# Decode block with cached attention: loops on four engines, another tail, and the query weights in eight transfers

## Chip, core and metric

The kernel runs on one NeuronCore of a Trainium2 chip. TensorE multiplies matrices into the eight banks of PSUM, VectorE (DVE) and ScalarE (ACT) work on SBUF and PSUM, GpSimd (POOL) makes a few constants, and SyncE (SP) issues almost all DMA transfers. Sixteen DMA engines move the data. The metric is the device time of one execution in microseconds (us).

## What is computed

One decoding step of a transformer block for two sequences: layer norm, attention of one query per head over a cache of 8192 keys and values, a residual, a second layer norm, a bilinear gated unit and another residual. All is float32.

```python
B, Sq, D = 2, 1, 448
H, Sk, Dh = 16, 8192, 256
F = 1792
q = (layernorm(x) @ wq).reshape(B, Sq, H, Dh).transpose(0, 2, 1, 3)
scores = einsum("bhqd,bhkd->bhqk", q, k_cache) * Dh ** -0.5
o = einsum("bhqk,bhkd->bhqd", softmax(scores), v_cache)
h = x + o.transpose(0, 2, 1, 3).reshape(B, Sq, H * Dh) @ wo
n = layernorm(h)
out = h + ((n @ w_gate) * (n @ w_up)) @ w_down
```

## The kernel before

There are 32 pairs of head and sequence, `NQ`, called heads here and numbered i. Each has 8192 keys and 8192 values of 256 floats. Partition p holds 64 consecutive keys, so a head's keys are one tile of 128 x 64 x 256 floats; so are its values. SBUF holds two key tiles (`k_sb`, even and odd heads) and one value tile (`v_sb`). Nothing is read twice, and there is no room for more of the cache.

**Start.** SP issues the query weights `wq` into the value tile (one transfer of 128 rows, L179), then head 0's keys in two pieces (16 and 48 of 64) and head 1's keys. ACT issues x. VectorE centres x, TensorE turns it, and TensorE projects the 4096 queries in eight groups of 512 columns, four matmuls each (L282), which ScalarE copies out with the norm's factor (L290). Between groups TensorE spreads the first two queries over 128 partitions with a matmul against ones (`spread_query`, L270). After the last group (`all_q`) the value tile is free, and SP issues head 0's values.

**Heads.** VectorE multiplies the keys in place by the spread query (L334) and sums over 256 columns (L337), in two pieces, then takes each partition's maximum (L381). TensorE turns these (`find_top`, L422), VectorE takes the largest (L343), TensorE spreads it (L426), and ScalarE takes the exponential with its sum (L352, L355). TensorE adds the sums up (L431), spreads the query of head i+2 (L270), mixes the values in 32 matmuls over four column groups (L413), and after ScalarE's copy (L363) turns the result (`turn_up`, L438); ScalarE scales it into `oT` (L365). Keys of head i+2 are issued when VectorE has done head i, values of head i+1 when TensorE has mixed head i. Only TensorE's heads stand in a loop (L446, 31 turns, `Fori`); VectorE, ScalarE and SP have their instructions written out one after another, and TensorE's last head too.

**Tail.** The output projection of 15 heads (`project_out`, L493, 60 matmuls over two halves of 224 columns) is done while the last values load. The last values come in 48 and 16 of 64. `sums` opens two sums in PSUM: `h_ps` for the norm and `y_ps` for the result. The last head's part is added to both (L589, L697), the total and the mean are taken (L597, L604), and the centred row is spread into `xr` (L630). Then follow the gate (L668 with `wg`), the up projection in two halves of its columns with `wu` (L668), each with its own product and flip (L717, L720, L727), and the down projection with `wd`, 14 rows of four matmuls (L738), loaded in pieces of 5, 5, 3 and 1 rows (`DOWN`). VectorE copies the result out (L747), SP stores it.

**What sets the order.** Each engine runs its instructions in the order in which they are written, and waits on counters (semaphores) of other engines and of loads. SP issues in its written order; DMA engines take transfers from its queue in that order.

Of the kernel before, what the change touches and what calls it, by code (L numbers as in the profile page):

```python
# [3 lines left out]
F32 = mybir.dt.float32  # L4
# [8 lines left out]
DC = 4  # L13
YN, YW = 4, D // 4
HW = D // 2
# [6 lines left out]
LASTV = 48  # L22
# [5 lines left out]
WIDE = [[min(n, (k + 1) * FH) - k * FH for n in FG] for k in range(2)]  # L28
PACKED = [3 * sum(n) + n[0] + n[2] for n in WIDE]
FF = [(n, g) for n in range(4) for g in range(4) if n < FG[g] // P]  # L30
DOWN = (5, 5, 3, 1)
# [8 lines left out]
class Line:  # L40


    def __init__(self, nc, engine, name):
        self.e = engine
        self.sem = nc.alloc_semaphore(name=name)
        self.n = 0
        self.seen = {}

    def wait(self, *tokens):
        for sem, n in tokens:  # L50
            if self.seen.get(sem.num, 0) < n:
                self.e.wait_ge(sem, n)
                self.seen[sem.num] = n

    def did(self, ins):
        ins.then_inc(self.sem, 1)
        self.n += 1
        return self.sem, self.n


class Tensor:


    def __init__(self, nc):
        self.e = nc.tensor
        self.sem = nc.alloc_semaphore(name="pe")
        self.n = 0
        self.parts = [(None, [])]

    def loop(self, *turns):  # L70

        self.parts.append((turns or None, []))

    def do(self, make, *waits, inc=False):
        self.parts[-1][1].append((make, waits, inc))
        if inc:
            self.n += 1
            return self.sem, self.n

    def emit(self):  # L80
        for turns, ops in self.parts:
            if turns:
                with self.e.Fori(*turns) as turn:
                    self.emit_part(ops, turn)
            else:
                self.emit_part(ops, None)

    def emit_part(self, ops, turn):
        seen = {}
        for make, waits, inc in ops:  # L90
            for w in waits:
                sem, n = w[:2]
                if len(w) == 3:
                    self.e.wait_ge(sem, turn * w[2] + n)
                elif seen.get(sem.num, 0) < n:
                    self.e.wait_ge(sem, n)
                    seen[sem.num] = n
            ins = make() if turn is None else make(turn)
            if inc:
                ins.then_inc(self.sem, 1)  # L100


def decode_block(nc, x, k_cache, v_cache, wq, wo, wg, wu, wd, out):
# [6 lines left out]
    bank = [nc.alloc_psum_tensor(f"bank{i}", [P, 512], F32)[:] for i in range(8)]  # L110
    first_sem = nc.alloc_semaphore(name="dve_first")
    V = Line(nc, nc.vector, "dve")
    A = Line(nc, nc.scalar, "act")
    A_q = Line(nc, nc.scalar, "act_q")
    G = Line(nc, nc.gpsimd, "pool")
    S = Line(nc, nc.sync, "sp")
    T = Tensor(nc)

# [3 lines left out]
    def load(line, dst, src, sem, n=16):  # L122
        line.e.dma_start(dst, src).then_inc(sem, 16)  # L123
        return sem, n
# [5 lines left out]

    room = {"at": 2 * NF * D}

    def late(*shape):

        n = 1
        for k in shape[1:]:
            n *= k
        at = room["at"]
        room["at"] += -(-n // 8) * 8
        assert room["at"] <= NJ * DH  # L140
        got = k_flat[1][: shape[0], at : at + n]
        names = "abcd"[: len(shape) - 1]
        if len(names) > 1:
            got = got.rearrange(
                f"p ({' '.join(names)}) -> p {' '.join(names)}",
                **dict(zip(names[1:], shape[2:])),
            )
        return got
# [8 lines left out]
    xr = sb("xr", P, DC + 1, B, 16)  # L157
    xz = sb("xz", P, DC + 1, B)
    sel = sb("sel", P, 2)
    rep = sb("rep", P, 2, B, REP)  # L160
    q_sb = sb("q_all", B, H * DH)

    s_x, s_wq, s_k0 = landing("x"), landing("wq"), landing("k0")
    s_k = [landing("k_even"), landing("k_odd")]
    s_v, s_v2 = landing("v"), landing("v_last")
    s_wo = [landing("wo_a"), landing("wo_b")]
    s_wg, s_wu = landing("wg"), [landing("wu_a"), landing("wu_b")]
    s_wd = [landing(f"wd{i}") for i in range(len(DOWN))]
    s_out = landing("out")

    def keys_of(cache, i, lo, hi):
        h, b = divmod(i, B)
        return cache[b, h].rearrange("(p j) d -> p j d", p=P)[:, lo:hi, :]

    x_in = load(A, x_sb, x.rearrange("b s d -> (b s) d"), s_x)
    wq_t = v_flat[:, : 3 * H * DH + H * DH // 2]
    wq_in = load(S, wq_t, wq, s_wq)  # L179
    k0_in = load(S, k_sb[0][:, :HC], keys_of(k_cache, 0, 0, HC), s_k0)  # L180
    k_in = {0: load(S, k_sb[0][:, HC:], keys_of(k_cache, 0, HC, NJ), s_k[0])}
    k_in[1] = load(S, k_sb[1], keys_of(k_cache, 1, 0, NJ), s_k[1])

    zero = G.did(nc.gpsimd.memset(ident, 0.0))
    G.wait(zero)
    ident_in = G.did(
        nc.gpsimd.affine_select(
            out=ident, in_=ident, compare_op=ALU.not_equal, fill=1.0, base=0,
            pattern=[[-1, P]], channel_multiplier=1,
        )  # L190
    )
    G.did(nc.gpsimd.memset(xz, 0.0))
    zeros_in = G.did(nc.gpsimd.memset(xr[:, DC - 1 :], 0.0))

    V.did(nc.vector.memset(eps_t, EPS))
    V.did(nc.vector.memset(ones, 1.0))
    V.did(nc.vector.memset(avg, 1.0 / D))
    V.did(nc.vector.memset(row, DH**-0.5))
    o_ps, h_ps, y_ps = bank[0], bank[5][:, :P], bank[6][:, :YW]
    V.wait(x_in)  # L200
    xsum = sb("xsum", B, 1)
    t = V.did(nc.vector.tensor_reduce(xsum, x_sb, axis=AX.X, op=ALU.add))
    V.wait(t)
    xmean = sb("xmean", B, 1)
    t = V.did(nc.vector.tensor_scalar(xmean, xsum, -1.0 / D, None, op0=ALU.mult))
    V.wait(t)
    xc_sb = sb("xc", B, DC * P)
    t = V.did(nc.vector.tensor_scalar(xc_sb[:, :D], x_sb, xmean, None, op0=ALU.add))
    V.wait(t)
    xc_in = V.did(nc.vector.tensor_copy(xc_sb[:, D:], xc_sb[:, D - HALF : D]))  # L210
    xq = o_sb[:B, :D]
    t = V.did(nc.vector.tensor_mul(xq, xc_sb[:, :D], xc_sb[:, :D]))
    V.wait(t)
    xvar = sb("xvar", B, 1)
    var_in = V.did(nc.vector.tensor_reduce(xvar, xq, axis=AX.X, op=ALU.add))

    std = sb("std", B, 1)
    A.wait(var_in)
    std_in = A.did(nc.scalar.activation(std, xvar, AF.Sqrt, bias=eps_t, scale=1.0 / D))
    rstd = sb("rstd", B, 1)  # L220
    V.wait(std_in)
    rstd_in = V.did(nc.vector.reciprocal(rstd, std))
    A.wait(rstd_in)
    A.did(nc.scalar.activation(std, std, AF.Exp, scale=0.0))

    xT_ps = bank[3][:, : DC * B].rearrange("p (c b) -> p c b", b=B)
    for c in range(DC):
        xT_in = T.do(
            lambda c=c: nc.tensor.transpose(
                xT_ps[:, c, :], xc_sb[:, c * P : (c + 1) * P], ident[:B, :B]  # L230
            ),
            ident_in, xc_in, inc=c == DC - 1,
        )
    V.wait(xT_in, zeros_in)
    for rows, c, to in LAYOUT:
        xz_in = V.did(nc.vector.tensor_copy(xz[rows, to], xT_ps[rows, c]))

    V.wait(ident_in)
    V.did(
        nc.vector.tensor_reduce(  # L240
            sel, ident.rearrange("p (g r) -> p r g", r=32)[:, :2, :], axis=AX.X, op=ALU.add
        )
    )
    V.did(
        nc.vector.tensor_copy(
            rep,
            ident.rearrange("p (k b) -> p k b", k=2)[:, :, :B, None].to_broadcast([P, 2, B, REP]),
        )
    )
    for ps in (o_ps, h_ps, bank[4][:, :HW]):  # L250
        set_in = V.did(nc.vector.memset(ps, 0.0))

    q_sel = sb("q_sel", B, DH)
    qb = [sb(f"qb{i}", P, DH) for i in range(2)]
    qb_ps = bank[1][:, :DH]
    q_ps = [bank[7][:B, :], bank[4][:B, :]]
    qsel_in, qb_in, Q_in = {}, {}, {}

    def select(i):
        h, b = divmod(i % NQ, B)  # L260
        if i > 0:
            A.wait(Q_in[i - 1])
        qsel_in[i] = A_q.did(
            nc.scalar.activation(  # L264
                q_sel, q_sb[:, h * DH : (h + 1) * DH], AF.Copy, scale=ident[:B, b : b + 1]
            )
        )

    def spread_query(*_):
        return nc.tensor.matmul(qb_ps, ones[:B, :], q_sel, start=True, stop=True)  # L270

    def take_query(i):
        A.wait(Q_in[i])
        qb_in[i] = A_q.did(nc.scalar.activation(qb[i % 2], qb_ps, AF.Copy))  # L274

    q_in = {}
    for g in range(NG):
        for c in range(DC):
            xs = c if c < DC - 1 else c + g // (NG // 2)
            at = c * H * DH + (g * QG if c < DC - 1 else g % (NG // 2) * QG)  # L280
            done = T.do(
                lambda g=g, c=c, xs=xs, at=at: nc.tensor.matmul(  # L282
# [11 lines left out]
        if g == 0:  # L294
            A.wait(q_in[0])
            select(0)
        if g == 1:
            Q_in[0] = T.do(spread_query, qsel_in[0], set_in, inc=True)
# [519 lines left out]
```

## Time and profile before

| | |
|---|---|
| median of 3 runs | 1302.37 us (1302.2 to 1302.61) |
| the profiled execution | 1301.42 us, of which the span from first to last instruction is 1300.1 us |
| bytes read | 561.19 MB, 432 GB/s over the span |
| granted TensorE clock, mean | 0.642 of full |
| first load issued | 0.73 us |
| projection of the queries done, first values issued | 53.66 us |
| last values issued | 1248.66 us |
| last down rows issued | 1275.74 us |

Times in the profile are in us from the span's start. Names such as `k` and `v` leave out the buffer's number. In the tail many small tiles lie in the key tiles, so they show as `k`; `v` stands for the value tile, which holds `wq` at the start and `wd` at the end. A float32 matmul shows as two entries of TensorE, and as two weight loads (PEld).

### The profile page before, as it was taken

Reading aid. Unit: us, or ns where it says so; the run is one execution under the profiler, and the core shown is the slowest. Engines: PE = TensorE matmul, PEld = TensorE weight load, DVE = VectorE, ACT = ScalarE, POOL = GpSimd, SP = SyncE. Lnnn points to the kernel's source line nnn. Section 1 sums busy time; section 2 is a strip of 40 time slices with the busy share of each in tenths; the row PEclk is TensorE's granted clock in tenths of the full one; section 3 lists DMA queues with packets and bytes.
Section 4 is the critical chain, followed back from the end, with each engine's and each line's share of the span. In section 5 each row is a group of like instructions: output and inputs, shape, how many; then the busy total and the mean of one; then the engine's idle time right before and its main releaser. Section 6 shows DMA issues by size and latency. Waiting matters only on the chain.

```text
span 1300.1 us, 6914 instructions
## 1 busy us (share of the span) xinstructions
PE 470.6 (36%) x2992; PEld 155.1 (12%) x2992; DVE 1131.2 (87%) x266; ACT 81.5 (6%) x239; POOL 0.8 (0%) x8
## 2 busy tenths in 40 slices
PE   3643224333323433322333322333321333432387
PEld 0111011101001101101101101101100110110123
DVE  1999998889888889888889988888988888988861
ACT  1100000000000000000000000000000000000000
POOL 0000000000000000000000000000000000000000
PEclk9866566666556666556666656666656666655689
DMA  9999999999999999999999999999999999999998
GB/s 411 427 450 421 450 421 444 426 436 436 421 450 421 448 423 448 423 446 425 442 427 427 444 421 450 422 446 425 446 423 446 425 440 429 427 444 423 446 421 367
DMA packets 10973, 561.31 MB, mean 432 GB/s; under 512 B 1234, under 2 KB 1364, under 8 KB 1492
## 3 DMA queue, kind: packets, MB, share of 16 engines
q1 hardware_dynamic: 10960, 561.19, 99.7%
q8 instruction: 5, 0.08, 0.0%
q14 instruction: 4, 0.03, 0.0%
q10 hardware_dynamic: 4, 0.00, 0.0%
HBM read 561.19 MB, written 0.00 MB: 432 GB/s over the span
## 4 chain that ended last, share of the span: by engine, by line
DMA 74%; PE 25%; issue 0%; ACT 0%; SPq 0%; DVE 0%
DMA v<-in_A_v_cache_dram 71%; PE bank L413 22%; PE bank L282 2%; DMA v<-in_wd_dram 2%; DMA v<-in_wq_dram 1%; PE bank L270 0%; SPq L123 0%; PE bank L738 0%; ACT q_all L290 0%; ACT q_sel L264 0%; DVE k L747 0%; ACT qb L274 0%
## 5 line engine op out<-in xcount | busy, mean ns | idle before, releaser
L334 DVE TENSOR_TENSOR k<-k,qb 128x4096 f32<-128x4096 f32 x64 | 555.3, 8676 | 124.2 <-DMA k<-in_A_k_cache_dram 95.9
L337 DVE TENSOR_REDUCE s<-k 128x16 f32<-128x4096 f32 x64 | 555.2, 8675 | 1.1
L413 PE MATMUL bank<-v,p 128*2 128x512 f32 x2048 | 291.4, 733 | 342.9 <-DMA v<-in_A_v_cache_dram 342.9
L413 PEld LDWEIGHTS bank<-v,p 128*2 128x2 f32 x2048 | 53.6, 96 | 573.4 <-DMA v<-in_A_v_cache_dram 365.9
L426 PE MATMUL bank<-nm,row 1*128 1x1 f32 x64 | 18.4, 354 | 227.6 <-DVE nm L343 227.6
L422 PE MATMUL bank<-ident,m 128*1 128x128 f32 x32 | 11.8, 368 | 184.4 <-DVE m L381 184.4
L363 ACT ACTIVATE o_sb<-bank 128x512 f32<-128x512 f32 x31 | 18.5, 597 | 604.0 <-PE bank L413 604.0
L426 PEld LDWEIGHTS bank<-nm,row 1*128 1x128 f32 x64 | 15.6, 302 | 236.9 <-DVE nm L343 236.9
L438 PE MATMUL bank<-sel,o_sb 128*128 128x1 f32 x256 | 33.7, 253 | 23.3 <-ACT o_sb L363 22.5
L270 PE MATMUL bank<-q_sel,ones 2*128 2x256 f32 x66 | 39.0, 691 | 1.4 <-ACT q_sel L264 1.4
L438 PEld LDWEIGHTS bank<-sel,o_sb 128*128 128x128 f32 x256 | 31.0, 191 | 53.1 <-ACT o_sb L363 51.5
L282 PE MATMUL bank<-v,xz 128*2 128x512 f32 x64 | 30.7, 639 | 16.0 <-DMA v<-in_wq_dram 16.0
L352 ACT ACTIVATE nb<-bank 128x1 f32<-128x1 f32 x32 | 5.5, 171 | 441.5 <-PE bank L426 441.5
L431 PE MATMUL bank<-lsum,ones 128*128 128x1 f32 x64 | 18.5, 359 | 23.5 <-ACT p L355 23.5
L422 PEld LDWEIGHTS bank<-ident,m 128*1 128x1 f32 x32 | 2.5, 79 | 188.2 <-DVE m L381 187.8
L431 PEld LDWEIGHTS bank<-lsum,ones 128*128 128x128 f32 x64 | 15.8, 306 | 26.2 <-ACT p L355 26.2
L270 PEld LDWEIGHTS bank<-q_sel,ones 2*128 2x128 f32 x66 | 15.9, 297 | 3.7 <-ACT q_sel L264 2.4
L264 ACT ACTIVATE q_sel<-q_all,ident 2x256 f32<-2x256 f32 x33 | 16.2, 492 | 0.0
L274 ACT ACTIVATE qb<-bank 128x256 f32<-128x256 f32 x32 | 12.2, 382 | 54.5 <-PE bank L270 54.5
L493 PE MATMUL bank<-k,oT 128*2 128x224 f32 x120 | 13.4, 387 | 0.0
L343 DVE TENSOR_REDUCE nm<-bank 1x1 f32<-1x128 f32 x32 | 8.7, 272 | 4.4 <-PE bank L422 4.4
L597 DVE TENSOR_REDUCE k<-bank 128x1 f32<-128x128 f32 x1 | 0.3, 292 | 13.1 <-PE bank L589 13.1
(81 smaller groups left out, 97.3 us busy)
## 6 DMA issues: line engine op xcount, KB each, us to landing
v<-in_wq_dram SPq DMA_DIRECT2D x1, 7168.0 KB, 19.5
k<-in_wo_dram SPq DMA_DIRECT2D x2, 3584.0 KB, 35.3
k<-in_A_k_cache_dram SPq DMA_DIRECT2D x1, 6144.0 KB, 38.0
v<-in_A_v_cache_dram SPq DMA_DIRECT2D x1, 6144.0 KB, 21.6
k<-in_wg_dram SPq DMA_DIRECT2D x1, 3136.0 KB, 28.0
v<-in_wd_dram SPq DMA_DIRECT2D x2, 1120.0 KB, 18.0
k<-in_A_k_cache_dram SPq DMA_DIRECT2D x1, 2048.0 KB, 23.9
v<-in_A_v_cache_dram SPq DMA_DIRECT2D x1, 2048.0 KB, 26.1
```

Of the source, the lines that this page charges most:

```text
L264: nc.scalar.activation(q_sel, q_sb[:, h * DH : (h + 1) * DH], AF.Copy, scale=ident[:B, b : b + 1])
L270: return nc.tensor.matmul(qb_ps, ones[:B, :], q_sel, start=True, stop=True)
L282: lambda g=g, c=c, xs=xs, at=at: nc.tensor.matmul(q_ps[g % 2], xz[:, xs, :], wq_t[:, at : at + QG], start=(c == 0), stop=(c == DC - 1),),
L334: t = V.did(nc.vector.tensor_mul(kt, kt, q[:, None, :].to_broadcast([P, hi - lo, DH])))
L337: V.did(nc.vector.tensor_reduce(s_t[i % 2][:, lo:hi], kt, axis=AX.X, op=ALU.add)),
L363: osb_in[i] = A.did(nc.scalar.activation(o_sb, o_ps, AF.Copy))
L413: lambda *_, t=t, g=g: nc.tensor.matmul(o_ps[g : g + 2, :], p_t[:, 2 * t : 2 * t + 2], v_sb[:, 2 * t : 2 * t + 2, :], start=(t < 4), stop= ...
L422: return T.do(lambda *_: nc.tensor.transpose(mT_ps, m_t, ident), m, inc=True)
L426: lambda *_: nc.tensor.matmul(nb_ps, row, nm, start=True, stop=True), nm_done, inc=True
L431: lambda *_: nc.tensor.matmul(l_ps, ones, lsum, start=True, stop=True), p_done, inc=True
L438: lambda *_, c=c, k=k: nc.tensor.matmul(oT_ps[:, c : c + 1], o_sb[:, (2 * k + c) * P : (2 * k + c + 1) * P], sel[:, k : k + 1], start=(k = ...
L493: lambda h=h, c=c, k=k: nc.tensor.matmul(acc_ps[HALF * k : HALF * k + B, :], oT[:, h, c, :], wo_c[:, h, c, k * HW : (k + 1) * HW], start=F ...
```

## The change

A class `Engine` takes the place of `Line` and `Tensor`. Work is recorded as a list for each engine, with names for what is waited for, and written out at the end. `roll` writes a body once with a loop around it; waits in it are against a register computed from the turn. `only` writes a block that is stepped over in all turns but one.

- **Loops.** TensorE: four turns over two query groups, then 32 turns over heads; the last head's extra work (`heads_out`) and one wait are blocks within the turn. VectorE: heads 1 to 30 as 15 turns of two. ScalarE: 16 turns of two. SP stays written out.
- **Query groups.** They run in the order 0, 4, 1, 5, 2, 6, 3, 7. The first query is spread inside the first turn, the second behind the loop.
- **Hints.** Each of SP, TensorE, ScalarE and VectorE gets a prefetch hint for code at its end, and a branch there that is never taken. TensorE has a second cut, `later()`, between gate and up projection: the far block gets a hint from the beginning, and is reached by a branch.
- **Query weights.** Eight transfers; transfer r holds rows r, r+8, ... of 128, sixteen rows of 57344 bytes.
- **Tail.** The 15 heads are projected 448 columns at a time over four column groups (30 matmuls and one for x); `sel` adds the groups into two halves, `half_ps`. Five filler matmuls (`keep_busy`) follow, ahead of the last mix. The last head is added to `half_ps` alone; ScalarE copies it with its row sum, and small matmuls make the centred row. The up projection runs over its full width, its loads cut by rows of the weights; the last chunk of gate and up takes 64 weight columns, in two matmuls where there were four. The first ten down rows are summed two rows high over four column groups (`part_ps`), with the residual; VectorE copies this, and four matmuls add it to `y_ps` beside the last four down rows. `DOWN` is 5, 5, 2, 1, 1. `wo` comes in one transfer, and all `wd` loads wait for the whole last mix.

```diff
-    wq_in = load(S, wq_t, wq, s_wq)
+    for r in range(8):
+        load(S, wq_t[r::8], wq[r::8], s_wq, "wq", n=8 * 16)
...
+    def emit(self, known):
+        e, nc, seen = self.e, self.nc, {}
...
+        hint = e.mark_branch_hint_location()
+        never = e.alloc_register(name + "never")
+        e.reg_mov(never, 0)
+        if self.split:
+            e.br_lt(never, 0, on_true=name + "far", on_false=name + "near").branch_hint(hint)
+            with nc.body(name + "near", valid_engines=here):
+                hint = e.mark_branch_hint_location()
+                self.emit_ops(self.items[self.ahead : self.split], known, seen)
+                nc.br(name + "far", engines=here)
+            nc.switch_bb(name + "far")
+        self.emit_ops(self.items[self.split or self.ahead :], known, seen)
+        e.br_lt(never, 0, on_true=name + "dead", on_false=name + "end")
+        with nc.body(name + "dead", valid_engines=here):
+            e.br_lt(never, 0, on_true=name + "dead", on_false=name + "end").branch_hint(hint)
...
+    def emit_turn(self, turns, steps, turn, known, seen):
+        for k, op in enumerate(turns[0]):
+            if op[0] == "only":
+                at = [j for j, t in enumerate(turns) if t[k][1]]
+                here = turn < steps[1] if at == [0] else turn > steps[-2]
+                with self.e.If(here):
+                    self.emit_ops(turns[at[0]][k][1], known, {})
+                continue
...
+                self.e.wait_ge(sem, turn * a + b if a else b)
...
+    T.roll(0, GH, 1, project_groups)
+    spread_query(1)
...
+    V.roll(1, NQ - 1, 2, lambda i: (scores(i), scores(i + 1)))
...
+    A.roll(0, H, 1, act_turn)
...
+    def heads_out():
...
+        for at in range(0, H - 1, 4):
+            for c in range(2):
+                for h in range(at, min(at + 4, H - 1)):
+                    g = 32 * (h % 4)
+                    T.do(
+                        lambda h=h, c=c, g=g: nc.tensor.matmul(
+                            acc_ps[g : g + B, :], oT[:, h, c, :], wo_c[:, h, c, :],
...
+        T.do(None, ("oT", NQ - 2))
+        T.roll(0, WARM, 1, keep_busy)
+    def keep_busy(_):
+        T.do(
+            lambda _: nc.tensor.matmul(warm_ps, ones, wo_t[:, : 2 * P], start=True, stop=True)
+        )
...
+        spread_query(i + 2)
+        T.only(last, heads_out)
+        at = 0
+        for k, n in enumerate(LAST):
+            if k > 0:
+                T.only(last, hold, ("v_last", k))
+            mix(
...
+    T.roll(0, NQ, 1, tensor_turn)
...
+    T.later()
+    project(u_ps, wu_t, lambda c: ("wu", c // 2), "u", "u_blank")
...
+    for k, (j, g) in enumerate(FF[:NPART]):
+        T.do(
+            lambda k=k, j=j, g=g: nc.tensor.matmul(
+                part_ps[32 * (k % 4) : 32 * (k % 4) + B, :],
+                hmT[:, j, 32 * g : 32 * (g + 1) : REP], wd_t[:, k, :],
+                start=(0 < k < 4), stop=(k >= NPART - 4),
+            ),
```

How the instructions now stand is shown at three places. First SP, from the top of the program: `v<-in_wq_dram` is the load of the query weights, the `k` loads are head 0's keys in two pieces and head 1's. Before:

```order
L123 DMA v<-in_wq_dram 128x14336
L123 DMA k<-in_A_k_cache_dram 128x4096
L123 DMA k<-in_A_k_cache_dram 128x12288
L123 DMA k<-in_A_k_cache_dram 128x16384
L123 DMA v<-in_A_v_cache_dram 128x16384
```

And with the change:

```order
L185 DMA v<-in_wq_dram 16x14336 x8
L185 DMA k<-in_A_k_cache_dram 128x4096
L185 DMA k<-in_A_k_cache_dram 128x12288
L185 DMA k<-in_A_k_cache_dram 128x16384
L95 BRANCH_PREFETCH_HINT
L185 DMA v<-in_A_v_cache_dram 128x16384
```

Seven more issues stand ahead of the keys, none ahead of the first weights; the hint stands behind the keys.

Second TensorE, one turn of the loop over heads. Before (`m`, `nm` and `lsum` belong to the softmax, `p` holds the exponentials):

```order
L422 MATMUL bank<-ident,m 1x128
L94 REGISTER_ALU
L426 MATMUL bank<-nm,row 128x1
L94 ISA
L431 MATMUL bank<-lsum,ones 128x1
L94 ISA
L270 MATMUL bank<-q_sel,ones 128x256
L94 ISA
L413 MATMUL bank<-v,p 2x512 x32
```

And with the change, from the spread query to the end of the mix:

```order
L379 MATMUL bank<-q_sel,ones 128x256
L139 COMPARE_AND_BRANCH
L553 MATMUL bank<-x,ident 2x448
L563 MATMUL bank<-k,oT 2x448 x30
L572 MATMUL bank<-k,sel 2x256
L572 MATMUL bank<-k,sel 2x192
L124 UNCONDITIONAL_BRANCH
L584 MATMUL bank<-k,ones 128x256
L124 REGISTER_ALU
L124 COMPARE_AND_BRANCH
L139 UNCONDITIONAL_BRANCH
L158 ISA
```

The sums over heads and the fillers, which stood behind the loop or nowhere, now lie inside the turn, between the spread query and the mix; 31 turns branch over them.

Third TensorE, the end of the program. Before (the second half of the up projection, its flips, the down projection):

```order
L668 MATMUL bank<-k,xr 32x256 x2
L668 MATMUL bank<-k,xr 32x128 x2
L720 MATMUL bank<-ident,k 128x128 x2
L668 MATMUL bank<-k,xr 32x256 x2
L668 MATMUL bank<-k,xr 32x128 x2
L668 MATMUL bank<-k,xr 32x256 x2
L668 MATMUL bank<-k,xr 32x128 x2
L720 MATMUL bank<-ident,k 128x128 x2
L738 MATMUL bank<-v,k 32x112 x56
```

And with the change:

```order
L722 MATMUL bank<-k,xr 32x384 x2
L733 MATMUL bank<-k,xr 64x512
L733 MATMUL bank<-k,xr 64x384
L766 MATMUL bank<-ident,k 128x128 x4
L783 MATMUL bank<-v,k 2x448 x10
L809 MATMUL bank<-v,k 32x112 x8
L799 MATMUL bank<-k,rep 32x112 x4
L809 MATMUL bank<-v,k 32x112 x8
```

Ten of the 14 down rows became one matmul each (L783), and a copy by VectorE now stands between them and L799; behind it come the last two rows, eight matmuls.

## Prediction before the run

> **What bounds the kernel.** I read the page first: shares, queues.
>
> ```profile
> span 1300.1 us, 6914 instructions
> ...
> PE 470.6 (36%) x2992; PEld 155.1 (12%) x2992; DVE 1131.2 (87%) x266; ACT 81.5 (6%) x239; POOL 0.8 (0%) x8
> ...
> q1 hardware_dynamic: 10960, 561.19, 99.7%
> ```
>
> VectorE is busy 87% of the span, but the data queue takes 99.7% of sixteen DMA engines' time. Next came the busy time by stage (stretch, its us, busy time of five engines, TensorE clock, DMA share, GB/s).
>
> ```profile
> 78.00:1238.00 1160.00, 386.54 (x2371) 126.36 (x2370) 1062.07 (x213) 67.31 (x210) 0.00 (x0) 0.61 1.00 434
> ...
> 1294.00:1295.00 1.00, 0.52 (x24) 0.28 (x12) 0.00 (x0) 0.00 (x0) 0.00 (x0) 1.00 0.93 384
> 1295.00:1296.00 1.00, 0.67 (x28) 0.68 (x32) 0.00 (x0) 0.00 (x0) 0.00 (x0) 1.00 0.69 274
> 1296.00:1297.00 1.00, 0.54 (x26) 0.30 (x19) 0.00 (x0) 0.00 (x0) 0.00 (x0) 1.00 0.29 113
> ```
>
> Over 1160 us of heads the share is 1.00 at 434 GB/s: 561.19 MB at that rate take 1293.1 us of a span of 1300.1 us. Only 7 us lie outside the stream, and the change moves the same bytes. So the question is what stands ahead of the stream, what behind it, and whether anything opens a hole. The chain of waits in order of time (start, us, what) shows both ends and the one tight place:
>
> ```profile
> 0.73 19.49 DMA v<-in_wq_dram
> ...
> 53.66 24.57 DMA v<-in_A_v_cache_dram
> ...
> 1277.04 19.87 DMA v<-in_wd_dram
> 1296.91 0.04 issue
> 1296.95 1.02 PE bank L738 x32
> 1297.97 0.03 issue
> 1298.00 0.28 DVE k L747
> ```
>
> **Part 1: the query weights in eight transfers.** The timeline of the start:
>
> ```profile
> 0.73 0.54 ACTq L123 DMA_DIRECT2D x<-in_A_x_dram  x1
> ...
> 1.19 1.46 SPq L123 DMA_DIRECT2D k<-in_A_k_cache_dram  x3
> ...
> 2.12 0.61 DVE L202 TENSOR_REDUCE xsum<-x 2x1 f32<-2x448 f32 x1 [0.96 <-DMA x<-in_A_x_dram]
> ```
>
> The weights are 128 rows of 14336 floats, 7.34 MB, at 434 GB/s 16.9 us; issue to landing was 19.49 us, so 2.6 us are ramp. A tiny load (x: issued 0.73, used 2.12) already takes 1.4 us, which no splitting removes, so at most 1.2 us can go. Eight issues at 1.46/3 = 0.49 us put the last at 0.73 + 3.4 = 4.1 us, and each piece moves for 16.9/8 = 2.1 us, so issuing stays ahead. The three key loads queued behind on SP go out 3.4 us later, long before the weights end. The smallest gain is none, and I allow a loss of 0.3 us, seven hand-overs of 0.04 us (the chain's "issue"). The tiny load says that most of the ramp is fixed: I take **-0.2 us** (-1.2 to +0.3).
> [...]
>
> **Part 2: the projection loop.** The first value load waits until the projection has read the weights, since both use one tile. It is the tight place: issued at 53.66 us, landed 24.57 us later. Its 8.39 MB take 19.3 us at 434 GB/s; with 1.4 us fixed, the queue held 3.9 us of work at the issue. If the new projection ends over 3.9 us later, the DMA engines stand idle.
>
> ```profile
> 20.32 9.78 PE L282 MATMUL bank<-v,xz 128*2 128x512 f32 x16 [16.02 <-DMA v<-in_wq_dram]
> ...
> 35.68 0.69 PE L270 MATMUL bank<-q_sel,ones 2*128 2x256 f32 x2 [1.43 <-ACT q_sel L264]
> 36.30 17.33 PE L282 MATMUL bank<-v,xz 128*2 128x512 f32 x40
> ```
>
> All 32 projections stay. The second query's spreading moves behind them, which takes a wait of 1.43 us and 0.69 us of work off this path, 2.1 us. Added are 32 address instructions and four loop ends, most of them beside 0.43 us matmuls (17.33/40); if all were exposed at 0.04 us, 1.4 us. So it ends 0.7 to 2.1 us earlier; as nothing waits for it while the queue is full, it is worth **0**. The bound on the other side is 3.9 us of delay, still 0.
>
> **Part 3: the loops over heads.** From the waits (total, times, longest), and from the DMA issues (median us to landing):
>
> ```profile
> DVE k L334 <- DMA k<-in_A_k_cache_dram: 95.9, 28, 3.9
> ```
> ```profile
> v<-in_A_v_cache_dram SPq DMA_DIRECT2D x31, 29.5
> ```
>
> VectorE waits 95.9/28 = 3.4 us for keys in nearly every head, and a value load is issued 29.5 - 19.3 - 1.4 = 8.8 us before the queue would run dry. So a head may cost VectorE 3.4 us more and TensorE 8.8 us more for nothing. Register instructions, loop ends and skipped blocks have no row. Between nothing and 0.49 us each, what a whole DMA issue takes on its sequencer, the dozen of VectorE's turn cost 0 to 6 us per two heads, under its cover of 6.8; TensorE's eight or so cost 0 to 4, under 8.8. **0**, with both ends covered. A cover that is exceeded costs 32 us for each us.
>
> **Part 4: code.** q8 and q14 fetch instructions on the same DMA engines. Their rows for 78 to 1238 us, then for 1259 to 1261, then for 1291 to 1294 (packets, MB, share of sixteen engines):
>
> ```profile
> q14 instruction: 4, 0.03, 0.0%
> q8 instruction: 1, 0.02, 0.0%
> ```
> ```profile
> q8 instruction: 1, 0.02, 2.7%
> ```
> ```profile
> q8 instruction: 1, 0.02, 1.9%
> ```
>
> 2.7% of 16 x 2 us is 0.86 us, 1.9% of 16 x 3 us is 0.91 us: one fetch takes one DMA engine 0.9 us that fifteen others don't lose, and a load lands with its slowest engine. The last DMA shares agree: before 1297 us they fall short by 0.07 + 0.31 + 0.71 = 1.1 us. Ending together, the engines would land the last piece 1.1 us earlier. The matmuls stored for TensorE fall from 316 to 162 (counted in the program), so fewer late fetches are due; but one engine with one fetch keeps the old end, and two on one engine end 0.9 us later. I take landings **0.4 us earlier** (1.1 earlier to 0.9 later).
>
> **Part 5: the tail.** From the timeline:
>
> ```profile
> 1260.12 0.19 ACT L355 ACTIVATION_READ_ACCUMULATOR p<-s,nb 128x1 f32 x1
> ...
> 1260.67 5.46 PE L493 MATMUL bank<-k,oT 128*2 128x224 f32 x56
> ...
> 1266.19 0.39 DVE L513 COPY k<-bank 128x224 f32<-128x224 f32 x1 [5.24 <-PE bank L493]
> ...
> 1270.35 7.05 PE L413 MATMUL bank<-v,p 128*2 128x512 f32 x64 [3.11 <-DMA v<-in_A_v_cache_dram]
> ...
> 1280.20 0.29 DVE L597 TENSOR_REDUCE k<-bank 128x1 f32<-128x128 f32 x1 [13.09 <-PE bank L589]
> ...
> 1282.59 3.29 PE L668 MATMUL bank<-k,xr 128*32 128x512 f32 x16 [1.22 <-DVE k L643]
> ...
> 1286.12 1.91 PE L668 MATMUL bank<-k,xr 128*32 128x512 f32 x16
> ...
> 1290.22 0.42 DVE L717 TENSOR_TENSOR k<-bank,k 128x256 f32<-128x256 f32 x1 [3.45 <-PE bank L668]
> ...
> 1295.33 0.92 PEld L738 LDWEIGHTS bank<-v,k 128*32 128x32 f32 x40 [1.05 <-DMA v<-in_wd_dram]
> ```
>
> Ahead of the last values: 28 old sums (56 entries, two column groups at once) took 5.46 us, 0.39 us per pair of 224 columns. All 60 took 11.7 us warm; the new 30 of 448 columns, four at once, are 8 rounds of 0.78 = 6.2 us. Those 5.5 us saved and the old wait of 3.1 us cover five fillers (256 columns: 0.45 us each warm, twice that cold). The last mix ran at full speed already (7.05 us for 64), so the fillers win nothing there: 0.
> Behind the mix, a ScalarE pass over 256 columns with its row sum (0.42 by VectorE's row of that width, + 0.19) stands where a 0.29 us reduction stood, then four small matmuls ahead of the mean: the gate starts 0.5 us later, at 1283.1. It takes 5.5 us as before (3.29, variance, 1.91), the up projection, of eight 0.43 us rounds as before, 3.4; product, flips and copies 1.3 (three of 0.42).
> At the end, the second down piece (landed by 1295.33) now feeds five 448-wide matmuls, two rounds or 1.56 us, then a 448-wide copy (0.39 + 224 x 0.03/32 = 0.60), four sums (8 entries of 1.02/32 us: 0.25) and two rows of four (0.5), with two hand-overs 3.0 us: **1298.3 us**, where 1297.97 stood. With landings 0.4 earlier, 1297.9: **-0.1 us**. The compute chain alone, 1283.1 + 5.5 + 3.4 + 1.3, ten partial rows in three rounds (2.3), copy and rest (1.4), gives 1297.0 and is just behind the data. So the bounds are -0.9 (the chain alone) and +1.2 (0.3 and landings 0.9 later). The output transfer stays.
>
> The profiled execution took 1301.42 us, 0.95 us under the median. 1301.42 - 0.2 - 0.1 = 1301.1, and 1302.37 - 0.3 = **1302.1 us**.
>
> **Rivals.**
> (1) *Slower: the loops' code does not stay in place.* TensorE's turn now steps over 31 sums and the fillers. If each of 32 turns fetched two blocks, 64 x 0.9 us on 16 engines delay the stream by 3.6 us: 1305.7 us. [...] Against: from 78 to 1238 us, thirty turns of TensorE's old loop, there is one q8 fetch. For: the new turn stores 74 matmuls where it stored 40.
> [...]
> (2) *Slower: one stall at the far code.* The up projection is reached by a branch right behind the gate. If its code isn't there, TensorE waits a fetch (0.9) and its way there (1.4, as for the tiny load) with little cover: 1304.4 us. The prefetch hint speaks against it.
> (3) *Slower: a hole at the start.* Eight pieces that don't overlap cost 7 x 1.4 = 9.8 us: 1311.9 us. Issues that stay ahead speak against it.
> (4) *Faster:* the whole ramp (1.2) and the tail's best (0.9): 1300.3 us; if the last values also land 1.1 us earlier, the compute chain moves with them: 1299.2 us.
>
> **How the numbers follow.** A measurement of this kernel can tell 0.2%, 2.6 us, from no change: below 1299.77 is faster, above 1304.97 slower. Forecast 0.72, (1) 0.06, (2) 0.08, (3) 0.04, (4) 0.10. Faster by over 0.2%: half of (4), 0.05. Slower: (1), (3) and 0.03 of (2), 0.13. Within: 0.82. The range takes the low bounds together (-2.1: 1300.3) and the high ones with (2) (1304.4); outside lie (1), (3), half of (4), the end of (2), 0.18.
>
> **What would show it.** Right: share 1.00 through the heads; weights landed 19 to 19.5 us after the first issue; the first value load issued near 52 us; VectorE still waiting for keys; the last copy, L819, within 1.5 us of the last landing. Wrong: dozens of q8 or q14 packets from 78 to 1238 us (1); TensorE idle at L722 with its weights landed (2); a share below 0.9 before 50 us (3); a last landing over 1.5 us earlier (4).

## The result and the profile after

| | before | with the change |
|---|---|---|
| median (runs) | 1301.97 us (6) | 1323.38 us (6; 1320.97 to 1323.94) |
| ratio to before | | 1.0159 [1.0148, 1.0169] |
| profiled execution, its span | 1301.42, 1300.1 us | 1323.94, 1322.4 us |
| queries' projection starts | 20.32 us | 39.54 us |
| first values issued | 53.66 us | 69.48 us |
| last copy of the result starts | 1298.00 us | 1320.17 us |

It became 1.6% slower, outside the range of 1300.3 to 1304.4 us. From the page after (share of the span; queues):

```profile
span 1322.4 us, 7262 instructions
...
PE 473.2 (36%) x2820; PEld 152.5 (12%) x2820; DVE 1132.6 (86%) x265; ACT 83.4 (6%) x245; POOL 0.8 (0%) x8
...
q1 hardware_dynamic: 11072, 561.19, 99.4%
q8 instruction: 1, 0.02, 0.0%
...
v<-in_wq_dram SPq DMA_DIRECT2D x8, 896.0 KB, 20.8
```

The data queue still takes 99.4% of the sixteen engines' time, yet the same bytes need 22 us more. The busy time by stage tells why (columns as in the prediction: TensorE clock, DMA share and GB/s last), after:

```profile
5.00:20.00 15.00, 0.00 (x0) 0.00 (x0) 2.44 (x10) 1.71 (x4) 0.00 (x0) 1.00 1.02 210
20.00:36.00 16.00, 0.00 (x0) 0.00 (x0) 0.00 (x0) 0.00 (x0) 0.00 (x0) 1.00 0.99 204
97.00:1257.00 1160.00, 386.79 (x2370) 126.12 (x2370) 1058.45 (x211) 67.28 (x210) 0.00 (x0) 0.61 1.00 434
```

and before, in the same first stretches:

```profile
5.00:20.00 15.00, 0.00 (x0) 0.00 (x0) 1.60 (x9) 1.59 (x3) 0.00 (x0) 1.00 0.91 394
20.00:36.00 16.00, 14.25 (x28) 2.75 (x28) 0.67 (x1) 3.20 (x6) 0.00 (x0) 1.00 1.06 457
```

While the queries' weights load, the share is 0.99 to 1.02, but the rate is 204 to 210 GB/s: the engines are busy all the time, and each byte takes twice as long. Through the heads nothing has changed (434 GB/s). The timeline of TensorE after, at both ends (start, us, line, count, idle time before and its releaser):

```profile
39.54 8.59 PE L388 MATMUL bank<-v,xz 128*2 x16 [35.22 <-DMA v<-in_wq_dram]
```
```profile
1287.39 2.43 PE L584 MATMUL bank<-k,ones 128*128 128x256 f32 x10
1289.75 7.05 PE L539 MATMUL bank<-v,p 128*2 128x512 f32 x64
...
1304.14 1.06 PE L722 MATMUL bank<-k,xr 128*32 128x512 f32 x3
...
1310.91 2.77 PE L722 MATMUL bank<-k,xr 128*32 128x512 f32 x24
```

The projection starts 19.2 us later. The last mix no longer waits for values, it stands right behind the fillers (L584); before, it waited 3.11 us. The first piece of these values had landed 1.3 us before the mix began (issued at 1266.3, 22.1 us to landing). And the gate, up to the start of the up projection, takes 1310.91 - 1304.14 = 6.8 us, where 5.5 stood. TensorE's clock is low there, while it is busy all the time:

```profile
1302.00:1305.00 3.00, 3.00 (x20) 2.06 (x24) 1.39 (x8) 0.00 (x0) 0.00 (x0) 0.50 1.00 425
1305.00:1310.00 5.00, 5.00 (x26) 1.67 (x20) 0.52 (x4) 0.00 (x0) 0.00 (x0) 0.59 1.00 423
```

The transfers' last slices after are these:

```profile
1314.00:1315.00 1.00, 0.68 (x4) 0.00 (x0) 0.26 (x1) 0.00 (x0) 0.00 (x0) 1.00 0.19 70
1315.00:1316.00 1.00, 0.77 (x4) 0.40 (x4) 0.80 (x3) 0.00 (x0) 0.00 (x0) 1.00 0.03 11
```

The stream is over near 1315, and the result is copied at 1320.17; before, it was over near 1297 and the copy stood at 1298.00. So there are two losses: one in the stream, one in the work behind it.

### The profile page after: what moved, and what is told of

Read it like the earlier page. It is cut to its first block, busy times and chain, and to the rows that moved or that the text cites. A ratio compares the mean times of both kernels' runs of the same rounds, so it can differ in the third digit from the quotient of the medians.

```text
span 1322.4 us, 7262 instructions
## 1 busy us (share of the span) xinstructions
PE 473.2 (36%) x2820; PEld 152.5 (12%) x2820; DVE 1132.6 (86%) x265; ACT 83.4 (6%) x245; POOL 0.8 (0%) x8
## 3 DMA queue, kind: packets, MB, share of 16 engines
q1 hardware_dynamic: 11072, 561.19, 99.4%
## 4 chain that ended last, share of the span: by engine, by line
DMA 50%; DVE 38%; issue 8%; PE 4%; SPq 0%; ACT 0%; DVEq 0%; another core or an unknown queue 0%; ACTq 0%
DMA k<-in_A_k_cache_dram 47%; DVE s L457 20%; DVE k L448 17%; DMA v<-in_wq_dram 3%; PE bank L388 1%; PE bank L563 1%; PE bank L722 1%; PE bank L539 1%; SPq L185 0%; DVE m L470 0%; DVE nm L476 0%; PE bank L584 0%; PE bank L783 0%; DVE rl L481 0%; PE bank L733 0%
## 5 line engine op out<-in xcount | busy, mean ns | idle before, releaser
L607 PEld LDWEIGHTS bank<-nm,row 1*128 1x128 f32 x64 | 15.9, 306 | 240.9 <-DVE nm L476 240.9
L388 PE MATMUL bank<-v,xz 128*2 x64 | 29.4, 618 | 35.2 <-DMA v<-in_wq_dram 35.2
L611 PE MATMUL bank<-lsum,ones 128*128 128x1 f32 x64 | 18.7, 362 | 23.5 <-ACT p L506 23.5
L416 ACT ACTIVATE q_sel<-q_all,ident 2x256 f32 (+1 forms) x35 | 17.2, 492 | 0.0
L388 PEld LDWEIGHTS bank<-v,xz 128*2 128x2 f32 x64 | 5.4, 87 | 57.7 <-issue 57.7
L506 ACT ACTIVATE p<-s,nb 128x64 f32<-128x64 f32 x32 | 11.1, 347 | 1.0
## 6 DMA issues: line engine op xcount, KB each, us to landing
v<-in_A_v_cache_dram SPq DMA_DIRECT2D x1, 6144.0 KB, 22.1
```

Of the source, the lines that this page charges most:

```text
L388: lambda turn, k=k, c=c, xs=xs, base=base: nc.tensor.matmul(q_ps[k], xz[:, xs, :], wq_t[:, bass.ds(turn * QG + base, QG)], start=(c == 0), ...
L416: return nc.scalar.activation(q_sel, q_sb[:, bass.ds(at, DH)], AF.Copy, scale=ident[:B, b : b + 1])
L607: lambda *_: nc.tensor.matmul(nb_ps, row, nm, start=True, stop=True),
L611: lambda *_: nc.tensor.matmul(l_ps, ones, lsum, start=True, stop=True),
```

## Experiments

Numbers with an interval are of 11 runs beside the kernel before; "one run" is a single time. Where a kernel's fence is one row, it is the busy time of the stretch named at its start.

### Which part costs it

**one_load**: the changed kernel, the weights in one transfer.

```diff
-    for r in range(8):
-        load(S, wq_t[r::8], wq[r::8], s_wq, "wq", n=8 * 16)
+    load(S, wq_t, wq, s_wq, "wq")
```

> The changed kernel with the query weights in one transfer of 128 rows again. If the eight transfers made the whole loss, the weights land 19 to 20 us after their issue (38.8 with the eight), and the time is that of the kernel before or under it, 1301 to 1302. If the new tail costs too, as its 7.5 us from the last landing to the end against 3.2 say, the time stays 1 to 4 us above the kernel before: 1303 to 1306.

1304.67 us (1302.36 to 1305.0), ratio 1.0016 [1.0007, 1.0025]. The row of the first stretch is that of before again:

```profile
5.00:20.00 15.00, 0.00 (x0) 0.00 (x0) 2.44 (x10) 1.67 (x4) 0.00 (x0) 1.00 0.92 399
```

So 1323.38 - 1304.67 = 18.7 us are the eight transfers, and 2 us are left for the rest of the change.

**before_eight**: the kernel before, with only this load in eight strided transfers.

```diff
-    wq_in = load(S, wq_t, wq, s_wq)
+    for r in range(8):
+        wq_in = load(S, wq_t[r::8], wq[r::8], s_wq, 8 * 16)
```

> The kernel before with nothing changed but the query weights in eight transfers of sixteen rows, eight apart. If the loads alone make 18.7 us (1323.4 less 1304.7): 1302.4 + 18.7, about 1321. If the stream's cover takes some of it where the rest of the kernel is as before: 1316 to 1320.

1321.32 us (one run), before 1301.73: 19.6 us more. The same loss without loops, hints or the new tail:

```profile
20.00:36.00 16.00, 0.00 (x0) 0.00 (x0) 0.00 (x0) 0.00 (x0) 0.00 (x0) 1.00 0.92 190
```

### Why the rate halves

Four kernels change only which rows of SBUF and which of memory a transfer of sixteen has. Where the two orders differ, the weights are stored in the other order, so that the result stays.

**rows_together** (neighbours on both sides), **apart_in_sbuf** (eight apart in SBUF, neighbours in memory), **apart_in_memory** (the other way round):

```diff
-        load(S, wq_t[r::8], wq[r::8], ...
+        load(S, wq_t[16 * r : 16 * r + 16], wq[16 * r : 16 * r + 16], ...
```
```diff
+        load(S, wq_t[r::8], wq[16 * r : 16 * r + 16], ...
```
```diff
+        load(S, wq_t[16 * r : 16 * r + 16], wq[r::8], ...
```

> Eight transfers still, but each of sixteen neighbouring rows, in SBUF and in memory. Theory A (the partitions written at one time, eight apart, share ways into SBUF) and theory B (the addresses read at one time, 448 KB apart, share ways out of memory): full rate, the weights landed by 21 us, about 1304. Theory C (a transfer of sixteen rows is slow as such): half rate as in the changed kernel, landed near 39 us, about 1323.

> Eight transfers; rows eight apart in SBUF, neighbouring in memory (the weights are packed in that order). Theory A and theory C: half rate, landed near 39 us, about 1323. Theory B: full rate, landed by 21 us, about 1304.

> Eight transfers; rows neighbouring in SBUF, eight apart (448 KB) in memory. Theory A: full rate, landed by 21 us, about 1304. Theory B and theory C: half rate, landed near 39 us, about 1323.

One run each: 1352.56, 1322.9 and 1351.62 us. Their rows, in that order:

```profile
20.00:36.00 16.00, 0.00 (x0) 0.00 (x0) 0.00 (x0) 0.00 (x0) 0.00 (x0) 1.00 1.01 115
```
```profile
20.00:36.00 16.00, 0.00 (x0) 0.00 (x0) 0.00 (x0) 0.00 (x0) 0.00 (x0) 1.00 0.94 194
```
```profile
20.00:36.00 16.00, 0.00 (x0) 0.00 (x0) 0.00 (x0) 0.00 (x0) 0.00 (x0) 1.00 1.00 115
```

The rate follows the rows of SBUF: eight apart 194 GB/s, neighbours 115, whatever the rows of memory. None of the three theories had foreseen that neighbours fall to a quarter.

**apart_by_two**: sixteen rows two apart, within 32.

```diff
+        rows = slice(32 * (r // 2) + r % 2, 32 * (r // 2) + 32, 2)
+        load(S, wq_t[rows], wq[rows], s_wq, "wq", n=8 * 16)
```

> Eight transfers of sixteen rows, two apart in SBUF, each within 32 partitions. Measured so far: 204 GB/s with rows eight apart, 115 with neighbours, 434 with all rows in one transfer. [...] Theory A2 (the rate grows with the distance between rows): between 115 and 204 GB/s, 45 to 60 us, 1328 to 1345. [...]

1324.62 us (one run), half the rate, as for eight apart:

```profile
20.00:36.00 16.00, 0.00 (x0) 0.00 (x0) 0.00 (x0) 0.00 (x0) 0.00 (x0) 1.00 0.94 194
```

**by_columns**: eight transfers of all 128 rows and an eighth of the columns, 896 KB each as in the change.

```diff
+    n = wq.shape[1] // 8
...
+        cols = slice(r * n, (r + 1) * n)
+        load(S, wq_t[:, cols], wq[:, cols], s_wq, "wq", n=8 * 16)
```

> Eight transfers of 896 KB again, but each of all 128 rows and an eighth of the columns. Theory A (what counts is which partitions are written at one time): full rate, over 420 GB/s, the weights landed by 21 us, about 1304.7 as with one transfer. A theory by which eight transfers or their size of 896 KB cost the rate: half rate, near 39 us, about 1323.

1305.46 us (one run), at the full rate:

```profile
5.00:20.00 15.00, 0.00 (x0) 0.00 (x0) 2.44 (x10) 1.69 (x4) 0.00 (x0) 1.00 1.03 434
```

So neither the number of transfers nor their size costs the rate.

**four_loads** and **four_together**: 32 rows each, four apart, and neighbouring.

```diff
+    for r in range(4):
+        load(S, wq_t[r::4], wq[r::4], s_wq, "wq", n=4 * 16)
```
```diff
+        load(S, wq_t[32 * r : 32 * r + 32], wq[32 * r : 32 * r + 32], s_wq, "wq", n=4 * 16)
```

> The changed kernel with the queries' weights in four transfers of 32 rows that lie four apart, instead of eight of 16 rows eight apart. Theory A1, a transfer reaches only the ways into the buffer that its rows lie on: 32 rows four apart lie on the same ways as 16 rows eight apart, so the rate stays at half, near 205 GB/s, the weights land near 39 us, and the time is near 1322 us. Theory N, few rows of one transfer are the cost: twice the rows, twice the rate, near 400 GB/s, the weights land near 21 us, and the time is near 1305 us.

> The changed kernel with the queries' weights in four transfers of 32 neighbouring rows, 0 to 31 first, instead of eight of 16 rows eight apart. Theory A2, the ways into the buffer follow from the row's number so that 16 neighbours share a quarter of them, 16 rows two or eight apart half, and 32 rows four apart, which ran at 400 to 462 GB/s, reach all: 32 neighbours reach as many as the 16 of them that lie two apart, half, so the rate is 194 to 210 GB/s, the weights land near 39 us, and the time is near 1322 us. Theory N, the rate follows from how many rows a transfer has (16 rows half, 32 rows all): 400 GB/s or more, landed near 21 us, 1305 us; the quarter of 16 neighbours would then be a case of its own.

One run each: 1304.96 us at the full rate, against the first expectation's theory of ways, and 1320.8 us at half:

```profile
5.00:20.00 15.00, 0.00 (x0) 0.00 (x0) 2.44 (x10) 1.68 (x4) 0.00 (x0) 1.00 0.93 400
```
```profile
20.00:36.00 16.00, 0.00 (x0) 0.00 (x0) 0.00 (x0) 0.00 (x0) 0.00 (x0) 1.00 0.93 190
```

With the same 32 rows a transfer, the rate is 400 or 190 GB/s: it is not how many rows, but which. Theory A2 of four_together gave the rate, 194 to 210 GB/s where 190 came; theory A1 of four_loads had given 205 for 32 rows four apart, where 400 came. What these theories call ways into the buffer was the author's assumption: the runs show the rates of rows, and no way as such. (The 462 GB/s given there for four_loads is its row of 20 to 36 us, when the weights had landed and keys were loading onto all 128 rows; the weights' own rate is the 400.)

While the weights load, the rate over all these kernels is 115 to 122 GB/s with sixteen neighbouring rows a transfer, 190 to 226 with sixteen rows two or eight apart or 32 neighbours, and 394 to 434 with 32 rows four apart or all 128. No other choice of rows was run.

### What else is lost, behind the last mix

**no_fillers**: one load, and the fillers left out, which feed no result.

```diff
-        T.roll(0, WARM, 1, keep_busy)
```

> One transfer for the query weights, and the filler matmuls left out. Theory F (the fillers stand in front of the last mix: it began at 1272.25 us right behind them, where the kernel before began it at 1270.35 with the landing): the mix starts at 1269.5 to 1270.5, the end comes 2 to 2.4 us earlier, about 1302.4, level with the kernel before. Theory G (the longer chain behind the mix is the whole loss, and the fillers keep TensorE fast for it): no gain or a loss, 1304.5 to 1306.

1302.65 us (1302.19 to 1303.17), ratio 1.0005 [0.9996, 1.0014]: theory F. That is 2.0 us under one_load's median. Each set against the kernel before of its own runs (1302.45 for one_load, 1301.73 here) they stand 2.2 and 0.9 us above it, so the fillers cost 1.3 to 2.0 us; the two intervals overlap, and the traces are the better witness. TensorE's timeline in one_load (ten entries of L583 are the five fillers):

```profile
1259.57 9.06 PE L562 MATMUL bank<-k,oT 128*2 128x448 f32 x60
1269.37 0.59 PE L571 MATMUL bank<-k,sel 128*2 128x256 f32 x4 [0.74 <-DVE k L498]
1269.89 2.42 PE L583 MATMUL bank<-k,ones 128*128 128x256 f32 x10
1272.25 7.05 PE L538 MATMUL bank<-v,p 128*2 128x512 f32 x64
```

and in no_fillers:

```profile
1269.83 7.05 PE L538 MATMUL bank<-v,p 128*2 128x512 f32 x64 [0.55 <-DMA v<-in_A_v_cache_dram]
...
1283.06 1.06 PE L720 MATMUL bank<-k,xr 128*32 128x512 f32 x3
...
1289.82 2.77 PE L720 MATMUL bank<-k,xr 128*32 128x512 f32 x24
```

The last row is the up projection, so the gate takes 6.8 us here too. The last values are there at 1269.8 in both (in one_load issued at 1247.0, 22.8 us to landing); with fillers the mix starts 2.4 us after that. They take exactly the time in which it could run. Where the slack went that was to cover them, the stages of one_load show:

```profile
1258.00:1260.00 2.00, 2.00 (x7) 0.18 (x10) 0.00 (x0) 0.77 (x2) 0.00 (x0) 0.50 0.96 418
1260.00:1265.00 5.00, 5.00 (x32) 1.04 (x28) 0.00 (x0) 0.00 (x0) 0.00 (x0) 0.50 1.07 462
1265.00:1266.00 1.00, 1.00 (x12) 0.19 (x8) 0.00 (x0) 0.00 (x0) 0.00 (x0) 0.80 0.23 98
```

and that of before in the like place:

```profile
1260.00:1266.00 6.00, 5.64 (x58) 2.77 (x58) 0.17 (x1) 0.31 (x2) 0.00 (x0) 1.00 0.93 401
```

The output projection runs at a clock of 0.50 up to some 1265.4 us, for 5.8 of its nine us. Before, the 28 sums of this stage ran at 1.00. Another 32 sums lay ahead of the softmax's matmuls there, and the stretch of low clock fell on those (0.50 from 1252 to 1254 us). In one_load TensorE has nothing to do in that place, until VectorE's maximum comes:

```profile
1254.27 0.37 PE L603 MATMUL bank<-ident,m 128*1 128x128 f32 x1 [5.51 <-DVE m L469]
```

That these 5.51 us of idle time are why the clock was low is the likely reading; no run here filled them.

**no_hints**: no_fillers, also without the hints and the far branch.

```diff
-        if self.ahead is None:
+        if True:
             return self.emit_ops(self.items, known, seen)
```

> The changed kernel with the queries' weights in one load, without the filler matmuls, and without the hints and the far branch ahead of the last stage's code. Theory H0, the hints are worth nothing here, since the short loops alone keep the fetches few and a fetch costs one DMA engine 0.9 us beside a stream of 1297 us: 1302.6 us, within 0.2% of the kernel of before, with 1 to 3 fetches on the page's instruction queue. Theory H1, a stall at the far code is what the hints save: TensorE or VectorE stands 1 us or more behind the last mix with nothing that it waits for, and the time is 1303.6 us or more.

1302.34 us (1301.84 to 1303.65), ratio 1.0 [0.9991, 1.0009]: H0. The page shows few fetches without hints too, four where no_fillers has one:

```profile
q8 instruction: 2, 0.03, 0.0%
q14 instruction: 2, 0.02, 0.0%
```

**gaps_filled**: one load; two fillers in each of TensorE's three gaps behind the last mix, none ahead of it.

```diff
+        T.only(last, keep_busy)
+        T.only(last, keep_busy)
...
+    for _ in range(2):
+        keep_busy()
     last_head()
+    for _ in range(2):
+        keep_busy()
```

> One load, and six filler matmuls of 256 columns, two in each of the three gaps of TensorE behind the last mix (0.72, 0.52 and 0.58 us in the kernel without fillers), where they stand ahead of nothing that is ready, in place of the ten ahead of the mix. Theory G, the clock of 0.50 to 0.78 between 1280 and 1288 us follows from those gaps: it stays at 1.00, the gate's matmuls take 4.0 us instead of 6.8, and the end comes 1.3 to 2.8 us earlier, 1300 to 1301.3 us. Theory W, the clock follows from how little the small matmuls of one to eight columns ask of TensorE over several us, and six fillers don't alter that: the clock falls as before, and the time is 1302.6 to 1303.2 us.

1302.46 us (1302.17 to 1302.81), ratio 1.0001 [0.9992, 1.001]: right of the clock, wrong of the time. The stage in no_fillers, and then stage and timeline in gaps_filled:

```profile
1280.00:1285.00 5.00, 4.42 (x28) 2.92 (x29) 1.75 (x10) 0.47 (x2) 0.00 (x0) 0.61 0.96 408
```
```profile
1280.00:1285.00 5.00, 5.00 (x42) 3.08 (x42) 1.75 (x10) 0.47 (x2) 0.00 (x0) 1.00 1.00 429
```
```profile
1283.91 1.91 PE L726 MATMUL bank<-k,xr 128*32 128x512 f32 x16
...
1288.05 1.91 PE L726 MATMUL bank<-k,xr 128*32 128x512 f32 x16
1290.39 1.05 PE L726 MATMUL bank<-k,xr 128*32 128x512 f32 x8 [0.42 <-DMA k<-in_wu_dram]
```

The gate takes 1288.05 - 1283.91 = 4.1 us in place of 6.8. But it starts 0.85 us later than in no_fillers, 0.6 of them because the last mix began later (1270.42 us), and the up projection, now early, waits for its weights; so does the down projection, 1.0 us for its second piece. The fillers here write another bank of PSUM than those ahead of the mix did.

**tail_order**: no_fillers; the residual's matmuls move behind the up projection's transposes, and the four that open the last sum to the very end.

```diff
-        if k == OPEN_AFTER:
-            open_sum()
+    open_sum()
```

> One load, no fillers, and two moves on TensorE's path behind the last mix: the four matmuls that add the residual (1.5 us ahead of and among the gate's) go behind the up projection's transposes, where TensorE waits for VectorE anyway, and the eight short matmuls that open the last sum (0.40 us) go to the very end, so that the other 28 of that sum run while VectorE copies (0.63 us). Theory P, the end hangs on TensorE's and VectorE's work behind the last mix: 0.7 to 1.5 us less than without fillers, 1301.1 to 1301.9 us. Theory D, it hangs on the last transfers, which don't move: 1302.6 us, no change.

1302.48 us (1301.52 to 1304.34), ratio 1.0004 [0.9995, 1.0013]: by the median, theory D. Its profiled execution, the shortest of the eleven, has the last copy 1.4 us earlier than no_fillers (1297.71, where 1299.08 stood):

```profile
1297.71 0.28 DVE L815 COPY k<-bank 128x112 f32<-128x112 f32 x1 [0.57 <-PE bank L797]
```
```profile
1299.08 0.27 DVE L817 COPY k<-bank 128x112 f32<-128x112 f32 x1 [0.91 <-PE bank L807]
```

The first row is tail_order, the second no_fillers. The median doesn't show that; why its runs spread over 2.8 us stays open.

**gaps_and_order**: both edits.

> One load, the six filler matmuls in TensorE's gaps behind the last mix, and the two moves of the order (the residual's matmuls behind the up projection, the opening of the last sum at the very end). With the fillers alone the clock stayed at 1.00 and yet the end came no earlier, with the order alone its best runs were 1301.5 us. Theory L, with both the work behind the last mix runs into the last transfers: TensorE waits for the up and down projections' weights, and the end follows their landing near 1296.3 us by some 3 us, so 1301.3 to 1302.4 us and no run below 1300.8 us. Theory C, the end still hangs on TensorE and VectorE: the two gains add, 1.3 us and 1.0 us, and the time is 1300.0 to 1300.9 us.

1301.78 us (1301.58 to 1302.42), before 1301.83, ratio 0.9999 [0.999, 1.0008]: theory L. From its waits of TensorE's weight loads (total us, times, longest):

```profile
PEld bank L719 <- DMA k<-in_wu_dram: 1.1, 1, 1.1
...
PEld bank L813 <- DMA v<-in_wd_dram: 0.5, 2, 0.3
PEld bank L787 <- DMA v<-in_wd_dram: 0.5, 1, 0.5
```

Both last projections wait for their weights, as in the kernel before. The new tail with these two losses mended ends where the old one did, right behind the stream.

## Why the prediction was wrong

**Part 1, the weights in eight transfers: wrong, and nearly the whole of the miss, 18.7 of 1323.38 - 1302.1 = 21.3 us.** The step that failed is "each piece moves for 16.9/8 = 2.1 us", which gave a piece of sixteen rows the rate of 128. At 204 GB/s its 0.918 MB take 4.5 us. The term was -0.2 us with +0.3 as its worst; it measured +18.7 to +19.6. Rival 3 had the right place and another mechanism, pieces that don't overlap, with 9.8 us as its price; and its sign, a share below 0.9, did not come in the stretches shown, since the share stayed at 0.99 to 1.02 while the rate fell. The trace of before has no load of sixteen rows, and that should have put the term's upper bound far beyond 0.3: a full-rate price was taken for an unseen kind of transfer. Its size of 896 KB is not the matter: by_columns has transfers of that size at 434 GB/s. Nor did the 1.2 us of ramp come where the rate stayed full: the projection starts at 20.64 us in by_columns and 20.93 in four_loads, 21.04 in one_load and 20.32 before (one execution each).

**Part 2, the projection loop: right to be free.** Without a hole behind it, the loop cost the stream nothing. The first values were issued 69.48 - 39.54 = 29.9 us after the projection began, 33.3 before: 3.4 us sooner, where 0.7 to 2.1 were given. In one_load, 52.04 - 21.04 = 31.0 us: 2.3 us sooner.

**Part 3, the head loops: right.** The rate through the heads is 434 GB/s on both sides, and VectorE still waits for keys (waits, after):

```profile
DVE k L448 <- DMA k<-in_A_k_cache_dram: 99.8, 30, 3.6
```

That is 3.3 us a head, where 3.4 stood. Rivals 1 and 2 fall: one q8 fetch in the whole execution, and no idle time ahead of L722 in the up projection.

**Part 4, code: right in kind; the size can't be told.** The fetches fell from nine to one. With the load undone, the last slice of the stream is emptier; one_load:

```profile
1296.00:1297.00 1.00, 0.73 (x4) 0.40 (x4) 0.80 (x3) 0.00 (x0) 0.00 (x0) 1.00 0.07 25
```

The share there is 0.07, where 0.29 stood. But slices of one us swing (1.70 from 1264 to 1265 us, 0.23 in the next), so neither this row nor the prediction's sum of three such slices, 1.1 us, says how much earlier the loads landed. The issues of the last rows of `wd` do. One_load (min, median and longest ns of an issue, first and last start; then us to landing):

```profile
L185 SPq DMA_DIRECT2D v<-in_wd_dram x5: 327/433/436, 1279.4 to 1281.3; - x5
DMA to landing us min/median/max: 12.9/15.8/15.9
```

The last piece landed near 1281.3 + 15.9 = 1297.2 us; before, near 1277.5 + 19.9 = 1297.4 (the 1275.74 us of the table ahead is the issue of the first of the four pieces). So some 0.3 us earlier, where 0.4 was given. That it comes so near may be luck: the same sum gives 1297.6 in no_hints, with four fetches, and 1297.9 in gaps_filled, with two. One execution of each doesn't tell what fetches, hints or later issues do here, and no_hints shows no difference in the time. That a fetch holds up one DMA engine of sixteen, and a load with it, was the author's estimate; no run shows it.

**Part 5, the tail: wrong by over 2 us.** It was given -0.1, and one_load stands 2.2 us above the kernel before. Two terms were mis-sized through the clock, which the sum did not follow. The output projection, "8 rounds of 0.78 = 6.2 us", took 9.06 us in one_load. Its 5.8 us at 0.50 and 3.2 us at 1.00 make 6.2 us of full clock: the rounds were right, the clock was not. So the 5.5 us "saved" were 2.6 at most. The fillers, which they were to cover, held back the mix by 2.4 us in one_load and by 1.3 us in the kernel with the change. The gate, "5.5 us as before", took 6.8. Before, the clock was at 0.50 from 1282 us to 1285.4, for 2.8 us of the gate; in no_fillers it was at 0.50 from 1281.1 us to 1287.5, for 4.4 us. With the gaps ahead of it filled, it took 4.1 at 1.00 (gaps_filled). A third term is the gate's start: it was 13.2 us behind the last mix's in no_fillers, where 12.2 stood, 1.0 later rather than 0.5. Without eight transfers and fillers the changed kernel is at a ratio of 1.0005, whose interval holds 1, though in its profiled execution the last copy starts 1.1 us later than before (1299.08 against 1298.00). gaps_and_order, at 0.9999, makes up for that and gains nothing beyond it.

## What to carry to other kernels

Here a transfer's rate went with the rows of SBUF which it touches. Of the cuts that were run, by columns with all rows in each piece (434 GB/s) and into 32 rows four apart (400) kept the rate; blocks of 16 and 32 neighbouring rows (115 and 190) and rows two or eight apart (194 and 204) did not; and no cut beat the single transfer (1305.46 and 1304.96 us, one run each, against 1304.67). Read GB/s beside the DMA share: in rows_together a share of 1.01 went with 115 GB/s, through the heads a share of 1.00 with 434. Fillers belong into gaps where nothing is ready; ahead of the last mix, whose values had landed, they pushed it back by 2.4 us in one_load. A price per matmul holds for the clock of the stage it was read from: the output projection, put at 6.2 us from matmuls at 1.00, took 9.06 in one_load with 5.8 us of it at 0.50. And where the last work waits for the stream, a faster clock bought nothing here: the gate took 4.1 us in place of 6.8 in gaps_filled, at 1302.46 us against no_fillers' 1302.65.

## What the runs showed of the hardware

- Sixteen neighbouring rows load at 115 to 122 GB/s, sixteen rows two or eight apart and 32 neighbours at 190 to 226, 32 rows four apart at 400, with a DMA share of 0.92 to 1.09 in all of them. Consecutive transfers on other rows of SBUF don't add up: in rows_together the next piece lies on other rows, and the rate stays 115.
- SP's issue of a transfer of sixteen rows eight apart took 5.04/8 = 0.63 us, of sixteen neighbouring rows (rows_together) 4.09/8 = 0.51, against 0.49 of the key loads before. 32 rows four apart take 2.48/4 = 0.62 at 400 GB/s (four_loads), 32 neighbours (2.11 - 0.74)/3 = 0.46 at 190 (four_together). Of eight transfers, the one that landed last was issued at 5.18 us with the change, 5.33 in apart_in_sbuf and 5.21 in apart_by_two, against 4.36 in by_columns. So in these runs the longer issues are those with a step between the rows of SBUF, whatever the rate:

```profile
0.73 5.04 SPq L185 DMA_DIRECT2D v<-in_wq_dram  x8
```
```profile
0.74 4.09 SPq L185 DMA_DIRECT2D v<-in_wq_dram  x8
```

- In the kernel before, SP's first three loads, issued from 0.73 to 2.65 us, landed in the order of their issue: 19.5, 23.9 and 38.0 us after it.
- TensorE's clock stayed at 0.50 from 1258 to 1265 us in one_load, though TensorE was busy all the time. Why it stayed low for over 7 us stays open.
- In the stage of small matmuls and short gaps behind the last mix the clock falls to 0.50 (before at 1282 us, in no_fillers at 1281.1, with gaps of 0.5 to 0.7 us); with two matmuls of 256 columns in each of three gaps it stayed at 1.00 (gaps_filled).
